# Chunked attention with a leaky-ReLU layer pair: two small VectorE operations in another form, value loads of two batches in pieces, and a new written order

## The chip, the cores and the metric

The kernel runs on one core of a Trainium2 chip. The time is that of the device for one launch, in microseconds, and the time of a kernel is the median of its runs. A profile is a separate, traced execution. The engines have these short names: PE is TensorE (PEld its weight loads), DVE is VectorE, ACT is ScalarE, POOL is GpSimd, SP is SyncE. In this kernel PE multiplies, DVE and ACT do the elementwise work, POOL does a part of it and issues the loads, and SP issues the stores and the DMA transposes.

## The reference

Eight batches of eight heads, 576 tokens and head dimension 64. Attention is local: each chunk of 64 tokens attends only to itself. The result, 4608 tokens by 512, goes through two matrix products with a leaky ReLU between them.

```
q_c, k_c, v_c = (t.reshape(B, H, 9, 64, 64) for t in (q, k, v))
scores = scale * np.matmul(q_c, k_c.transpose(0, 1, 2, 4, 3))
scores = scores - np.max(scores, axis=-1, keepdims=True)
attn = np.exp(scores)
attn = attn / (np.sum(attn, axis=-1, keepdims=True) + 1e-09)
out = np.matmul(attn, v_c)
x = out.transpose(0, 2, 1, 3).reshape(4608, 512)
h = x @ w_in          # 512 x 2048
g = np.maximum(0.01 * h, h)
return g @ w_out      # 2048 x 512
```

All numbers come in and go out as float32; the kernel computes in float16 with float32 sums.

## The kernel before

**Units and blocks.** Attention runs in 36 units of 128 tokens (two chunks, eight heads each); a unit is called u. The two products run in 19 blocks of tokens, called j: two of 128 tokens, then 17 of 256. The units feed a ring of transposed attention results, xT, and a block starts when its tokens are there. The second product of a block of 256 (and from block 14 on the first one too) is made by a scheme with seven products of half size instead of eight: that needs sums of inputs (SG, line 230, of the hidden values; TW, line 206, and WS, line 401, of the weights; xs, line 425, of the tokens) and sums of results (line 318).

**Stages of a unit.** Each unit passes through a chain. Its q and k come in (line 100), and are transposed: by PE for the first units, by DVE from unit 14 on, and by a DMA transpose that SP issues from unit 27 on (KT in line 843, QT in line 849; a DVE copy in line 856, stage cq, then spreads QT into the zero-padded tile QZ). Stage s (line 866) multiplies q and k into the scores Sp. Stage m (line 875) takes the maximum. Then there are two ways. Stages b and x subtract the maximum on DVE (line 880) and take one exponential on ACT (line 912). Stages nb and f scale the maximum by -1/8 on DVE (line 889) and take eight exponentials on ACT with that as their bias (line 897), which give the sums as well. UB lists the units from 14 on that go the first way. Stage z adds 1e-9 to the sums (line 924) and inverts them (line 926), stage n multiplies (line 932, on POOL from unit 10 on), stage d transposes the result by a DMA that SP issues (et, line 955), stage v multiplies by the values (line 966), and stage a (line 980, ACT) writes xT.

**Values.** The values of a batch lie in one of two tiles, VB0 and VB1, in every other block of a zero-padded square. The last unit that reads a batch issues the load of the batch after the next (lines 973 and 974), as two DMAs on POOL's queue.

**What sets the order.** Every engine executes its instructions in the order in which the program issues them; there is no scheduler behind it. For the first six units that order is written out in the string FRONT. It names stages and, as A and B, pieces of the first two blocks' products; as H their activation; as i matmuls on a tile of ones that fill waiting time; as y and w the zeroing of tiles. A third number after q, or a second one after k and c, says which of DVE and ACT makes the copy. Behind the front, the products are a list of pieces (chunks), issued one after the other; every other stage is an event with a due step, counted in pieces, which comes from base offsets (T and SPACE for the scores, VO for stage v, O_A and O_B for loads and DMA transposes) plus a shift from the table MOVED. Events that are due are issued ahead of the next piece. SG_POOL, XS_POOL and LEAK_DVE say which single sums and activations go to another engine than the usual one. Buffers come from rings: QT and q_in share a ring of five.

## Time and profile before

| what | value |
|---|---|
| median of 3 runs | 280.67 us (279.67 to 282.15) |
| the profiled execution's own time | 282.5 us |
| its span, first to last instruction | 280.7 us |
| PE busy | 270.9 us |
| DVE, ACT, POOL busy | 227.1, 190.3, 149.2 us |
| granted TensorE clock | 1.0 in all slices |

Times within the profile are counted from the start of the span. In a row of the order of time the first number is the start, the second the time taken, both in us, and a bracket at the end tells how long the engine stood idle ahead of the instruction and what ended that. Ends of matmuls are modelled, and a group of eight matmuls of 256 columns, listed with 1.04 us, is followed by the next group 0.87 us after its own start; the time that PE loses is therefore read from start to start. Rows of the table of stretches give busy time of PE, PEld, DVE, ACT and POOL, with the number of instructions, then the granted clock, the DMA share and GB/s.

### The profile page before, as it was taken

Reading aid. Unit: us, or ns where it says so; the run is one execution under the profiler, and the core shown is the slowest. Engines: PE = TensorE matmul, PEld = TensorE weight load, DVE = VectorE, ACT = ScalarE, POOL = GpSimd, SP = SyncE. Lnnn points to the kernel's source line nnn. Section 1 sums busy time; section 2 is a strip of 40 time slices with the busy share of each in tenths; the row PEclk is TensorE's granted clock in tenths of the full one; section 3 lists DMA queues with packets and bytes.
Section 4 is the critical chain, followed back from the end, with each engine's and each line's share of the span. In section 5 each row is a group of like instructions: output and inputs, shape, how many; then the busy total and the mean of one; then the engine's idle time right before and its main releaser. Section 6 shows DMA issues by size and latency. Waiting matters only on the chain.

```text
span 280.7 us, 8516 instructions
## 1 busy us (share of the span) xinstructions
PE 270.9 (96%) x3464; PEld 242.6 (86%) x3464; DVE 227.1 (81%) x453; ACT 190.3 (68%) x485; POOL 149.2 (53%) x176
## 2 busy tenths in 40 slices
PE   8889999999999999999999999999898999999995
PEld 4569958999999998999989999999788989999994
DVE  5876599899787988899968686779789989675684
ACT  6766734766657768657897646567566978976751
POOL 8838646879376696968232734268065472530000
PEclk9999999999999999999999999999999999999999
DMA  9999999999999999997919999999999423120213
GB/s 147 148 189 178 207 176 156 154 125 114 83 108 155 74 105 130 136 163 59 175 24 133 114 172 265 196 103 185 128 170 143 114 41 96 21 77 0 77 40 112
DMA packets 173958, 35.02 MB, mean 125 GB/s; under 512 B 164960, under 2 KB 169440, under 8 KB 173920
## 3 DMA queue, kind: packets, MB, share of 16 engines
q0 software_dynamic: 140256, 18.23, 113.2%
q1 hardware_dynamic: 32624, 16.00, 27.0%
q8 instruction: 27, 0.44, 0.6%
q10 hardware_dynamic: 1040, 0.26, 0.4%
q14 instruction: 11, 0.09, 0.1%
HBM read 36.96 MB, written 9.44 MB: 165 GB/s over the span
## 4 chain that ended last, share of the span: by engine, by line
PE 82%; DMA 8%; issue 4%; DVE 3%; POOL 2%; SPq 0%; POOLq 0%; DVEq 0%
PE hT L356 30%; PE prX L254 19%; PE prZ L254 6%; PE pr L254 6%; PE xbank L457 6%; PE xpr L457 4%; DMA VB<-in_v_dram 3%; PE prW L254 3%; PE Sp L866 3%; PE xp L966 3%; PE oP L503 2%; DMA k_in<-in_k_dram 2%; DMA et<-en 1%; DMA QT<-q_in 1%; DVE QZ L856 1%
## 5 line engine op out<-in xcount | busy, mean ns | idle before, releaser
L356 PE MATMUL hT<-xT,w_inT 128*128 128x256 f16 (+1 forms) x1088 | 103.1, 247 | 0.6 <-DMA w_inT<-in_moe_w_in_dram 0.6
L356 PEld LDWEIGHTS <-w_inT 128*128 128x128 f16 x1088 | 84.2, 98 | 7.2 <-issue 0.8
L370 ACT ACTIVATE gT<-hT 128x512 f16<-128x512 f32 x104 | 61.5, 605 | 26.2 <-PE hT L356 26.1
L932 POOL TENSOR_TENSOR en<-ex,zi 128x512 f16<-128x512 f16 x26 | 28.0, 1079 | 69.1 <-ACT gT L370 14.6
L254 PEld LDWEIGHTS <-SG 128*128 128x128 f16 x544 | 51.4, 98 | 5.4
L254 PEld LDWEIGHTS <-gT 128*128 128x128 f16 x400 | 37.7, 98 | 4.1
L254 PE MATMUL prX<-TW,SG 128*128 128x256 f16 x272 | 35.2, 273 | 0.0
L875 DVE TENSOR_REDUCE mx<-Sp 128x8 f32<-128x512 f32 x36 | 24.7, 685 | 12.2 <-PE Sp L866 12.0
L297 ACT ACTIVATE keep<-prX 128x256 f32<-128x256 f32 x51 | 19.9, 391 | 19.2 <-PE prX L254 18.9
L494 DVE TENSOR_TENSOR xkeep<-xpr,xkeep 128x512 f32<-128x512 f32 x30 | 19.9, 683 | 10.2 <-PE xpr L457 6.3
L100 POOL DMA_DIRECT2D q_in<-in_q_dram x25 | 21.1, 849 | 12.9 <-DMA QT<-q_in 6.4
L897 ACT ACTIVATE ex<-Sp,nb 128x64 f16<-128x64 f32 x80 | 24.0, 329 | 5.4 <-DVE nb L889 5.3
L980 ACT ACTIVATE xT<-xp 128x512 f16<-128x512 f32 x36 | 21.7, 602 | 5.5 <-PE xp L966 5.5
L100 POOL DMA_DIRECT2D k_in<-in_k_dram x25 | 20.6, 827 | 7.9 <-DMA VB<-in_v_dram 3.4
L230 DVE TENSOR_TENSOR SG<-gT 128x1024 f16<-128x1024 f16 x33 | 22.8, 692 | 1.0 <-ACT gT L370 0.8
L115 POOL DMA_DIRECT2D q_d<-in_q_dram x24 | 19.9, 830 | 2.2 <-DVE QZ L824 1.6
L486 ACT ACTIVATE xkeep<-xbank 128x512 f32<-128x512 f32 x30 | 16.8, 596 | 5.4 <-PE xbank L457 5.3
L115 POOL DMA_DIRECT2D k_d<-in_k_dram x24 | 19.5, 813 | 1.5 <-DMA k_d<-in_k_dram 1.1
L922 DVE TENSOR_REDUCE z<-ex 128x8 f32<-128x512 f16 x26 | 17.6, 677 | 2.9 <-ACT ex L912 2.6
L457 PEld LDWEIGHTS <-WS 128*128 128x128 f16 x320 | 19.3, 98 | 0.4
L122 POOL DMA_DIRECT2D VB<-in_v_dram x16 | 18.7, 1178 | 1.1 <-PE xp L966 1.1
L824 DVE STREAM_TRANSPOSE QZ<-q_d 64x512 f16<-64x512 f16 (+1 forms) x28 | 18.2, 655 | 0.3
(99 smaller groups left out, 486.9 us busy)
## 6 DMA issues: line engine op xcount, KB each, us to landing
out_dram<-osb SPq DMA_DIRECT2D x35, 256.0 KB, 3.5
VB<-in_v_dram POOLq DMA_DIRECT2D x16, 288.0 KB, 7.4
q_in<-in_q_dram POOLq DMA_DIRECT2D x19, 128.0 KB, 6.8
k_in<-in_k_dram POOLq DMA_DIRECT2D x19, 128.0 KB, 6.8
w_inT<-in_moe_w_in_dram POOLq DMA_DIRECT2D x8, 256.0 KB, 7.6
w_outT<-in_moe_w_out_dram POOLq DMA_DIRECT2D x4, 512.0 KB, 11.1
q_d<-in_q_dram POOLq DMA_DIRECT2D x24, 72.0 KB, 4.9
k_d<-in_k_dram POOLq DMA_DIRECT2D x24, 72.0 KB, 5.0
```

The source lines that it names most:

```text
L100: nc.gpsimd.dma_start(out=to, in_=rows)
L115: nc.gpsimd.dma_start(out=t[p0:p0 + 32, m, :, :, :].rearrange("p h b d -> p (h b) d"), in_=src[b, h0:h0 + 2, :, dh * 32:dh * 32 + 32].rear ...
L230: (nc.gpsimd if (j, n) in SG_POOL else nc.vector).tensor_tensor(out=SG[j, n], in0=x, in1=y, op=op)
L254: nc.tensor.matmul(out=to[:, i, :], lhsT=left[:, f, i * 128:(i + 1) * 128], rhs=right[:, f, :], start=(j, where) not in opened, stop=(f == ...
L297: nc.scalar.activation(out=half(kept[j, n]), in_=half(bank[j, "X"]), func=AFT.Copy, bias=0.0, scale=1.0)
L356: nc.tensor.matmul(out=hT[:, i, :], lhsT=w_inT[:, t, fc * 128:(fc + 1) * 128], rhs=xT[:, t, r0:r0 + tb], start=(t == 0), stop=(t == NT - 1),)
L370: nc.scalar.activation(out=gT[j][:, nf * a:nf * a + nf, c0:c0 + tb], in_=HT.pop((j, a, p)), func=AFT.Prelu, bias=0.0, scale=1.0, alpha=0.01,)
L457: nc.tensor.matmul(out=to[:, i, :], lhsT=left[:, t, i * 128:(i + 1) * 128], rhs=right[:, t], start=(n in (1, 2, 5) and t == 0 and i == 0), ...
L875: nc.vector.tensor_reduce(out=MX[u], in_=SP[u], axis=AXL.X, op=ALU.max)
L897: nc.scalar.activation(out=E[u][:, i, :], in_=SP[u][:, i, :], func=AFT.Exp, bias=NB[u][:, i:i + 1], scale=SCL, accum_out=Z[u][:, i:i + 1],)
L932: (nc.gpsimd if u >= UP else nc.vector).tensor_tensor(out=E[u], in0=ex, in1=ZI.pop(u).unsqueeze(2).to_broadcast((128, 8, CH)), op=ALU.mult)
L980: nc.scalar.activation(out=xT[:, :, at:at + G], in_=xp, func=AFT.Copy, bias=0.0, scale=1.0)
```

## The change

There are five parts.

1. Stage nb multiplies the maximum by a tile of 128x8 that holds -1/8 (minus), and stage z adds a tile that holds 1e-9 (tiny). Both were operations of a tensor and a number, and both are now operations of two tensors. Two small memsets at the start fill the tiles.
2. Unit 16 goes the first way (b, x) instead of the second (nb, f).
3. The values of batches 2 and 7 are loaded by four DMAs of half the size, as events of their own with the name vl, 2.5 steps apart and shifted by MOVED; the others are loaded as before.
4. The string FRONT is another one, and in the list of first loads unit 1 comes ahead of unit 2, and the fourth quarter of w_out ahead of the second.
5. The tables and offsets that set the due steps have other numbers. Two more sums SG go to POOL, the four xs of block 17 go from POOL to DVE, and two more activations go to DVE.

The added `need` and `made` lines are checks while the program is built; they issue nothing.

```diff
-    UB = (15, 17, 18, 19, 24, 25, 26, 27, 28, 30, 32, 34)
+    VL = (2, 7)
+    VS = 2.5
+    UB = (15, 16, 17, 18, 19, 24, 25, 26, 27, 28, 30, 32, 34)
...
+    def load_v_heads(b, m, h0, h1):
+        nc.gpsimd.dma_start(
+            out=VB[b % NVB][m * CH:(m + 1) * CH, h0:h1, :, m * CH:(m + 1) * CH].rearrange("p h c d -> p (h c) d"),
+            in_=v[b, m * H // 2 + h0:m * H // 2 + h1].rearrange("h (c j) d -> j (h c) d", j=CH),
+        )
...
+    tiny = sbp.tile([128, 8], FP32, name="tiny")
+    nc.vector.memset(tiny, 1e-9)
+    minus = sbp.tile([128, 8], FP32, name="minus")
+    nc.vector.memset(minus, -SCL)
...
-        "g2 g1 g3 v0 Q0 Q1 g4 Q2 Q3 g5 P0 P1 P3 P2 g6 v1 g7 g8 "
+        "g1 g2 g3 v0 Q0 Q1 g4 Q2 Q3 g5 P0 P3 P1 P2 g6 v1 g7 g8 "
...
-    MOVED = {..., 'WS 3': 3.25, 'd 30': 0.5, 'tdq 32': -0.5, 'tdq 33': 0.75, 'tdk 29': 0.25, 'tdk 33': 1.0, ...}
+    MOVED = {..., 'WS 3': 9.25, 'd 30': 6.25, 'tdq 32': 2.5, 'tdq 33': 5.25, 'tdk 29': 3.25, 'tdk 33': -1.5, ..., 'tdq 30': -3.0, 'vl 7 3': -2.0, 'vl 2 0': -1.0, ...}
-    SG_POOL = ((14, 1), (14, 4))
+    SG_POOL = ((14, 1), (14, 4), (16, 4), (17, 1))
...
-        nc.vector.tensor_scalar_mul(out=NB[u], in0=MX.pop(u), scalar1=-SCL)
+        nc.vector.tensor_tensor(out=NB[u], in0=MX.pop(u), in1=minus, op=ALU.mult)
...
-        nc.vector.tensor_scalar_add(out=ze, in0=z, scalar1=1e-9)
+        nc.vector.tensor_tensor(out=ze, in0=z, in1=tiny, op=ALU.add)
...
             if c == NCH - 1 and b + NVB < B:
-                load_v(b + NVB)
+                if b + NVB in VL:
+                    for i in range(4):
+                        later(i * VS, "vl", b + NVB, i)
+                else:
+                    load_v(b + NVB)
...
+    def load_v_piece(b, i):
+        made.add(("vl", b, i))
+        load_v_heads(b, i % 2, i // 2 * H // 4, i // 2 * H // 4 + H // 4)
...
 (FRONT, the pieces behind the first of block 0)
-  A0.0 H0.0 A1.0 e2 H1.0 A1.1 c2 v2 tq4 tk4 q4.0 H1.1 A0.1 a2 k4 H0.1 A2.0
+  A0.0 k3.1 z2 n2 A1.0 s3 H0.0 e2 c2 H1.0 A1.1 v2 A0.1 tq4 m3 tk4 H1.1 a2 A2.0
...
-    O_A = 12.0
-    O_B = 15.0
+    O_A = 10.0
+    O_B = 16.0
```

Three places of the order are shown, from the stretch between units 28 and 31. First POOL's, before the change: there en is a unit's attention (stage n), q_in and k_in are the loads of units 32 and 33, and VB1 is the load of batch 7.

```order
L100 DMA q_in_3756<-in_q_dram 128x8x64
L100 DMA k_in_3758<-in_k_dram 128x8x64
L932 TENSOR_TENSOR en_3787<-ex_3733,zi_3785 128x512
L122 DMA VB1_64<-in_v_dram 64x36x64 x2
L932 TENSOR_TENSOR en_3897<-ex_3831,zi_3883 128x512
L100 DMA q_in_3899<-in_q_dram 128x8x64
L100 DMA k_in_3901<-in_k_dram 128x8x64
L932 TENSOR_TENSOR en_4047<-ex_4015,zi_4032 128x512
```

With the change the same place on POOL reads so:

```order
L948 TENSOR_TENSOR en_3785<-ex_3733,zi_3783 128x512
L102 DMA q_in_3787<-in_q_dram 128x8x64
L102 DMA k_in_3789<-in_k_dram 128x8x64
L123 DMA VB1_64<-in_v_dram 64x18x64 x2
L948 TENSOR_TENSOR en_3887<-ex_3832,zi_3873 128x512
L123 DMA VB1_64<-in_v_dram 64x18x64
L102 DMA q_in_3912<-in_q_dram 128x8x64
L102 DMA k_in_3914<-in_k_dram 128x8x64
L123 DMA VB1_64<-in_v_dram 64x18x64
L948 TENSOR_TENSOR en_4049<-ex_4015,zi_4033 128x512
```

The load of unit 32 has moved behind the attention of unit 28, and the values stand in four rows of half the size, the third ahead of and the fourth behind the load of unit 33.

Second SP's queue, before the change, up to the transpose of k of unit 33; et is a unit's transposed attention (stage d: units 28, 29 and 30 here), osb2 a store of results, and the first KT and QT are those of unit 31.

```order
L330 DMA out_0_dram<-osb2_3714 128x512
L330 DMA out_0_dram<-osb2_3689 128x512
L955 DMA_TRANSPOSE et_3811<-en_3787 128x4x128
L843 DMA_TRANSPOSE KT_3813<-k_in_3614 128x4x128
L849 DMA_TRANSPOSE QT_3837<-q_in_3611 128x4x128
L955 DMA_TRANSPOSE et_3903<-en_3897 128x4x128
L843 DMA_TRANSPOSE KT_3979<-k_in_3758 128x4x128
L849 DMA_TRANSPOSE QT_3994<-q_in_3756 128x4x128
L330 DMA out_0_dram<-osb2_3992 128x512
L955 DMA_TRANSPOSE et_4091<-en_4047 128x4x128
L330 DMA out_0_dram<-osb2_3895 128x512
L843 DMA_TRANSPOSE KT_4141<-k_in_3901 128x4x128
```

With the change:

```order
L344 DMA out_0_dram<-osb2_3718 128x512
L860 DMA_TRANSPOSE KT_3777<-k_in_3629 128x4x128
L344 DMA out_0_dram<-osb2_3691 128x512
L971 DMA_TRANSPOSE et_3811<-en_3785 128x4x128
L866 DMA_TRANSPOSE QT_3813<-q_in_3626 128x4x128
L971 DMA_TRANSPOSE et_3899<-en_3887 128x4x128
L860 DMA_TRANSPOSE KT_3993<-k_in_3789 128x4x128
L866 DMA_TRANSPOSE QT_4035<-q_in_3787 128x4x128
L344 DMA out_0_dram<-osb2_3988 128x512
L860 DMA_TRANSPOSE KT_4064<-k_in_3914 128x4x128
L344 DMA out_0_dram<-osb2_3885 128x512
L971 DMA_TRANSPOSE et_4180<-en_4049 128x4x128
```

The transpose of k of unit 31 has moved ahead of a store and of unit 28's attention, and that of k of unit 33 and a store now stand ahead of unit 30's attention. Further ahead, the two transposes of unit 30 have moved before unit 27's attention.

Third DVE, before the change, up to the copies of QT of unit 31 (COPY QZ1); mx and Sp are those of unit 30.

```order
L401 TENSOR_TENSOR WS3_3937<-w_inT_68 128x2x512 x2
L425 TENSOR_TENSOR xs_3951<-xT_70 128x256
L875 TENSOR_REDUCE mx_3962<-Sp_3953 128x8
L401 TENSOR_TENSOR WS4_3964<-w_inT_68,WS2_3843 128x2x512 x2
L425 TENSOR_TENSOR xs_3951<-xs_3951,xT_70 128x256
L880 TENSOR_TENSOR Sp_3953<-Sp_3953,mx_3962 128x512
L318 TENSOR_TENSOR osb2_3992<-prZ_3920,keep_3990 128x256
L425 TENSOR_TENSOR xs_3951<-xT_70 128x256
L856 COPY QZ1_66<-QT_3837 64x8x64 x2
```

With the change:

```order
L416 TENSOR_TENSOR WS3_3951<-w_inT_68 128x2x512 x2
L416 TENSOR_TENSOR WS4_3954<-w_inT_68,WS2_3842 128x2x512 x2
L891 TENSOR_REDUCE mx_3966<-Sp_3957 128x8
L332 TENSOR_TENSOR osb2_3988<-prZ_3922,keep_3986 128x256
L896 TENSOR_TENSOR Sp_3957<-Sp_3957,mx_3966 128x512
L440 TENSOR_TENSOR xs_3991<-xT_70 128x256
L873 COPY QZ1_66<-QT_3813 64x8x64 x2
L440 TENSOR_TENSOR xs_3991<-xs_3991,xT_70 128x256
```

Both sums of weights now stand ahead of the maximum of unit 30, and one sum xs stands ahead of the copies instead of three. On PE the scores of unit 31 have moved one piece ahead and stage v of unit 29 one piece back; stages v of units 6, 8, 9, 13, 19, 23 and 25 stand one to three pieces earlier, and those of units 20, 27 and 28 one piece later.

More of the change, by code (lines that the diff above doesn't have):

```diff
@@ L216, in token_sums @@
             return
+        if j in EARLY:
+            for a, p in {
+                1: [(a, 1) for a in range(4)], 2: [(0, 2), (1, 2)], 3: [(0, 1), (1, 1), (0, 2), (1, 2)], 4: [(2, 2), (3, 2)],
+            }[n]:
+                need("act", j, a, p)
         if n in (2, 4):
@@ L794, in stage_q @@
             of = of.rearrange("p i e (r j) -> p (i e) r j", r=2)
+        need("zero", u % NQZ)
+        made.add(("dq", u, s))
         if act:
@@ L960, in stage_v @@
     def stage_v(u):
+        for i in range(2):
+            need("zero", NQZ + 2 * ((2 * u + 1) // NCH % NVB) + i)
         et = ET.pop(u)
@@ L972, in stage_v @@
                 )
+            if b in VL:
+                for i in range(4):
+                    need("vl", b, i)
             if c == NCH - 1 and b + NVB < B:
-                load_v(b + NVB)
+                if b + NVB in VL:
+                    for i in range(4):
+                        later(i * VS, "vl", b + NVB, i)
+                else:
+                    load_v(b + NVB)
         XP[u] = xp
+    def load_v_piece(b, i):
+        made.add(("vl", b, i))
+        load_v_heads(b, i % 2, i // 2 * H // 4, i // 2 * H // 4 + H // 4)
     def stage_a(u):
@@ L1007, in second_layer @@
     def second_layer(j, p):
+        need("act", j, p, 0)
         chunks.remove(("mm2", j, 0, p))
```

32 lines of the change are left out of this document (16 added, 16 removed), and 14 rows, old and new, of the table FRONT.

## The prediction

> **What bounds the kernel now.** I read the busy times first, then stretches of the span, then the order of time on PE, and from each wait there back to DVE, SP and POOL.
>
> ```profile
> PE 270.9 (96%) x3464; PEld 242.6 (86%) x3464; DVE 227.1 (81%) x453; ACT 190.3 (68%) x485; POOL 149.2 (53%) x176
> ```
>
> ```profile
> 100.00:120.00 20.00, 20.00 (x221) 18.07 (x220) 17.86 (x34) 13.64 (x39) 17.15 (x21) 1.00 2.43 138
> 200.00:220.00 20.00, 17.50 (x247) 15.93 (x245) 16.25 (x36) 14.67 (x42) 9.75 (x12) 1.00 1.31 141
> 240.00:260.00 20.00, 20.00 (x276) 18.74 (x274) 12.91 (x25) 15.44 (x32) 6.19 (x9) 1.00 0.11 35
> 270.00:281.00 11.00, 7.50 (x81) 6.65 (x78) 6.40 (x13) 2.58 (x6) 0.00 (x0) 1.00 0.28 97
> ```
>
> PE works 96% of the span at the full granted clock, and in the stretches 100 to 120 and 240 to 260 it never stops. So the kernel is PE's list of pieces plus the places where PE stands still: the front, the stretch 200 to 220, and the last three microseconds, when the products are done and only additions and stores are left. The change leaves PE's products as they are (one filler matmul more), so it can gain only at places where PE stands still, and it loses wherever it makes a new one. In the stretch 200 to 220 PE's order of time shows three stops.
>
> ```profile
> 201.18 1.04 PE L356 MATMUL hT<-xT,w_inT 128*128 128x256 f16 x8
> 203.37 0.41 PE L866 MATMUL Sp<-KT,QZ 128*128 128x64 f16 x8 [1.16 <-DVE QZ L856]
> 204.32 0.41 PE L966 MATMUL xp<-et,VB 128*128 128x64 f16 x8 [0.54 <-DMA et<-en]
> ...
> 211.63 1.04 PE L254 MATMUL prZ<-TW,SG 128*128 128x256 f16 x8
> 213.47 0.41 PE L866 MATMUL Sp<-KT,QZ 128*128 128x64 f16 x8 [0.80 <-DVE QZ L856]
> ```
>
> Eight matmuls of 256 columns hold PE for 0.87 us and eight of 64 columns for 0.24. From start to start the scores of unit 31 therefore lose 203.37 - 201.18 - 0.87 = 1.32, stage v of unit 29 loses 204.32 - 203.37 - 0.24 = 0.71, and the scores of unit 32 lose 213.47 - 211.63 - 0.87 = 0.97: 3.0 us together. The first and the third wait for the copies of QT (line 856), the second for the transposed attention et. Next, what DVE waited for there, and SP's queue.
>
> ```profile
> 200.58 0.29 DVE L425 TENSOR_TENSOR xs<-xT 128x256 f16<-128x256 f16 x1
> 202.73 0.59 DVE L856 COPY QZ<-QT 64x512 f16<-64x512 f16 x2 [1.86 <-DMA QT<-q_in]
> ...
> 211.60 1.81 DVE L856 COPY QZ<-QT 64x512 f16<-64x512 f16 x2
> ```
>
> ```profile
> 190.33 1.22 SPq L955 DMA_TRANSPOSE et<-en  x1
> 191.72 1.25 SPq L843 DMA_TRANSPOSE KT<-k_in  x1
> 193.14 1.27 SPq L849 DMA_TRANSPOSE QT<-q_in  x1
> 194.88 1.62 SPq L955 DMA_TRANSPOSE et<-en  x1
> ...
> 205.75 1.20 SPq L955 DMA_TRANSPOSE et<-en  x1
> 207.04 0.53 SPq L330 DMA_DIRECT2D out_dram<-osb  x1
> 207.67 1.81 SPq L843 DMA_TRANSPOSE KT<-k_in  x1
> ```
>
> ```profile
> 186.61 0.95 POOL L100 DMA_DIRECT2D q_in<-in_q_dram  x1 [1.52 <-DMA QT<-q_in]
> ...
> 190.26 2.37 POOL L122 DMA_DIRECT2D VB<-in_v_dram  x2
> ```
>
> ```profile
> QT<-q_in SPq DMA_TRANSPOSE x9, 4.6
> ```
>
> The transpose QT of unit 31 was issued at 193.14 and DVE got it at 202.73, 9.6 us later, against a median of 4.6 for its kind. The et of unit 29 went out at 194.88 and released PE at 204.32, 9.4 us later. Both follow the value load of batch 7, issued at 190.26. So the hole is a load of values that stands in the way of transposes which PE needs soon.
>
> **The change part by part.** All times are in the clock of the profiled execution: its span of 280.7, and 1.8 around it to its own 282.5. That is 1.8 above the median of 280.67, so I take the sum as a difference and subtract it from the median.
>
> *The front.* Its rows on PE:
>
> ```profile
> 20.00 0.39 PE L940 MATMUL tpe<-ident,en 128*128 128x128 f16 x4
> 20.77 1.05 PE L356 MATMUL hT<-xT,w_inT 128*128 128x128 f16 x16 [0.38 <-DMA w_inT<-in_moe_w_in_dram]
> 21.66 0.40 PE L966 MATMUL xp<-et,VB 128*128 128x64 f16 x8
> 21.89 0.39 PE L771 MATMUL qp<-ident,q_in 128*128 128x128 f16 x4
> 22.57 0.38 PE L771 MATMUL kp<-ident,k_in 128*128 128x128 f16 x4 [0.29 <-DMA k_in<-in_k_dram]
> ```
>
> The start of the hidden products is set by loads (w_in at 20.77, k of unit 4 at 22.57), and those loads keep their places in the queue; the swaps are of equal sizes. So whatever is reordered before 20.77 costs and brings nothing as long as it is done by then: the scores of unit 3 now stand in the wait ahead of 20.77. The transposes of q and k of unit 4 now stand behind the piece A0.1, so the stop 22.57 - 21.89 - 0.23 = 0.45 has work in it. Bounds: -0.45, and 0 if the attention of unit 2, which now has one copy of k more ahead of it on DVE, comes late instead. I take -0.35. From there to 200, PE stops nowhere, so this gain is carried.
>
> *The hole.* The transposes of unit 31 are due about one and a half steps earlier. KT now stands ahead of unit 28's attention, so that QT follows the latter's issue (190.33 + 1.22) at about 191.6 in place of 193.14, and behind it only half of the values have been put in the queue. If QT takes as long as before, 9.6, it lands at 201.2; with the median of 4.6 it lands at 196.2. DVE had reached this point at 200.58 + 0.29 = 200.87 and loses two of the three small sums ahead of it, so the copies can run from 200.3 and end at 200.9. The scores now stand one piece ahead, at 201.18 of the old clock less the front's 0.35, that is 200.8. Their loss is then 0.1 to 1.2; I take 0.2, near the median's end, because the copies need QT only at 200.3, 8.7 us after its issue: 1.1 less than before.
>
> Stage v of unit 29 goes behind two pieces: 200.8 + 0.2 + 0.24 + 2 x 0.87 = 203.0. Its et goes out as before at 194.88 less 0.35, because its attention on POOL does; with 9.4 it comes at 203.9 and costs 0.9, with less it costs nothing. I take 0.3 in place of 0.71.
>
> The scores of unit 32 come 7.1 after the next pieces' start on PE's list, in both kernels. The copies ahead of them took 1.81 for what takes 0.59 above. Their chain begins with the scores of unit 31 and runs over nb, so all of it moves up by the same 2.4 or so; without the 1.2 of slowness they don't hold PE, with it they hold it as before. I take 0.25 in place of 0.97, as the copies now come before POOL's sums of the tokens of block 15, which wait for the attention of unit 29.
>
> New costs: the et of unit 28 has a transpose more ahead of it in SP's queue, but it is used one piece later; and the et of unit 30 stands behind the load of k of unit 33. I put 0.2 for both, from 0 to what the slow rival below gives.
>
> *The two-tensor forms.* These rows bound them:
>
> ```profile
> 220.40 1.29 DVE L889 TENSOR_SCALAR nb<-mx 128x8 f32<-128x8 f32 x1
> ...
> 249.56 1.12 DVE L230 TENSOR_TENSOR SG<-SG,gT 128x1024 f16<-128x1024 f16 x1
> ```
>
> ```profile
> L230 DVE TENSOR_TENSOR SG<-gT 128x1024 f16<-128x1024 f16 x33 | 22.8, 692 | 1.0 <-ACT gT L370 0.8
> ```
>
> ```profile
> 219.54 2.12 POOL L230 TENSOR_TENSOR SG<-gT 128x1024 f16<-128x1024 f16 x1
> ...
> 249.47 0.66 POOL L425 TENSOR_TENSOR xs<-xT,xs 128x256 f16<-128x256 f16 x1
> ```
>
> The nb at 220.40 took 1.29 and ended when POOL's sum ended (221.66). If the new form never waits, this saves at most about 1.1 at that place. But the sum at 249.56, already an operation of two tensors in SBUF, ran 1.12 beside a POOL operation as well, 0.4 more than the mean of 0.69 of the sums like it. So I take 0 for the edit on PE's path. The Trainium skill, page "SBUF — State Buffer", section "Who interferes with whom", says of this that a VectorE instruction with two SBUF inputs contends with a GpSimd instruction that reads SBUF, though not with one that only writes it; by that rule the new form escapes descriptor writing alone, the sum stays as it is, and the trace agrees (1.12 at 249.56).
>
> *The rest.* Unit 16 on the other way gives DVE two more operations over a unit's scores and takes seven operations from ACT; it lies near 105, where DVE has 20 - 17.86 = 2.1 us to spare, room for two of up to 1 us each, and PE never stops: 0. The value load of batch 2 in pieces is read 30 us later: 0. The moves in blocks 16 and 17 lie where DVE is busy 12.91 of 20: 0. If that cover fails, the new sum on POOL (2.12 by the row above, against 0.69) holds up block 18's sums by up to 1.4; I leave it in the range.
>
> Sum: -0.35 (front) - 1.1 - 0.4 - 0.7 (hole) + 0.2 = -2.35. From its own time 282.5 that is 280.15, from the median 280.67 it is 278.3.
>
> **The rivals.** *All stops close.* With the median latency the hole's 3.0 and the front's 0.45 go whole and nothing new comes: 280.67 - 3.45 = 277.2, and somewhat less if later small stops go too. For it: 4.6 is the usual. Against it: loads of unit 32 now fall into the same stretch.
>
> *The crowd stays.* The load of unit 32 was issued at 186.61 and now follows the attention of unit 28, at 190.3, into the crowd, which is what half the values have left. QT then lands as before, at 202.73 - 0.35, its copies end at 203.0, and the scores, now one piece ahead, stop PE for 2.2 in place of 1.32; stage v loses nothing (-0.71), unit 32 loses as before: -0.35 + 0.9 - 0.7 = -0.15, so 280.5.
>
> *Slower: SP stands still for k of unit 33.* Its transpose (207.67 before, behind the et of unit 30 at 205.75) now stands ahead of that et, and its load stands behind three of the four value pieces. Stage v of unit 30 reads that et here:
>
> ```profile
> 216.37 0.40 PE L966 MATMUL xp<-et,VB 128*128 128x64 f16 x8
> ```
>
> In the new clock that is 216.37 - 2.5 = 213.9. Issued behind the transpose (1.81) and a store (0.53), and with QT's 4.6 to land, the et is late once the transpose goes out after 207.0; the gain is eaten once it goes out after 209.3. If the load comes 3 us later than 207.67, PE stops there for 3.7, and the sum is +1.35: 282.0. Against it: at 207.67 at the latest that load had landed, with all four pieces ahead.
>
> *The front or a moved stage v slips.* Seven stages v stand 0.87 to 2.6 earlier, and the front's DVE chain is fuller. One stop of 1.2 gives 279.5.
>
> **How the numbers follow.** Chances: the forecast 0.50 (own range 277.2 to 279.4), all stops close 0.17, the crowd stays 0.15, SP stands still 0.10, a stage slips 0.08. The likeliest gives 278.3. The range from 276.6 to 281.0 takes in all but the slow rival and the ends of the others. One per cent, about what a measurement can tell here (the three runs spread over 0.9%), is 2.8 us: faster than 277.86 are two fifths of the forecast's cases and the first rival, 0.36; slower than 283.5 are half of the slow rival's cases and a few of the last, 0.07; the rest, 0.57, is within.
>
> **What would show it.** The hole's step is right if the scores of unit 31 and 32 and stage v of unit 29 show waits under 0.3 each, and QT of unit 31 is there when DVE comes. It is wrong if DVE again waits over 1 us for QT. The front is right if no transposition of k waits near 22. The slow rival shows as a wait of stage v for et near 214 behind a late KT in SP's queue. The two-tensor step is wrong if nb never takes over 0.3 beside POOL's sums. The whole is wrong if PE loses more than 0.5 at any place between 25 and 195.

## The result, and the profile after

The changed kernel takes 279.13 us, the median of 20 runs (278.31 to 280.82); the kernel before, run beside it on the same chip, 281.72 (20 runs, 279.67 to 285.39). The ratio is 0.9915, with a 95% interval of 0.9892 to 0.9937: 1.8 to 3.0 us less. That is within one per cent, the most likely of the three outcomes in the prediction. The profiled execution of the changed kernel has a time of 279.04 and a span of 277.3; 280.7 was the span before. So the two profiles lie 3.4 apart and the medians 2.6; where the 0.8 comes from is seen below.

The busy times, and the four stretches that the prediction reads (length, busy time of PE, PEld, DVE, ACT and POOL, granted clock, DMA share, GB/s):

```profile
PE 269.9 (97%) x3465; PEld 242.7 (88%) x3465; DVE 227.9 (82%) x460; ACT 186.9 (67%) x468; POOL 153.6 (55%) x178
```

```profile
100.00:120.00 20.00, 20.00 (x215) 18.04 (x214) 17.93 (x35) 11.91 (x23) 15.79 (x19) 1.00 2.36 136
200.00:220.00 20.00, 19.90 (x289) 18.38 (x288) 17.88 (x40) 18.05 (x57) 11.38 (x12) 1.00 1.16 151
240.00:260.00 20.00, 19.94 (x276) 18.68 (x274) 15.73 (x28) 13.57 (x28) 7.23 (x6) 1.00 0.23 58
270.00:277.30 7.30, 4.04 (x45) 3.55 (x43) 3.24 (x9) 0.77 (x2) 0.00 (x0) 1.00 0.30 108
```

From 200 to 220 PE now works 19.90 of 20 where it worked 17.50. At 100 and at 240 it does not stop, as before, and the end (products done, stores left) is as long as it was. The hole on PE's order of time in the changed kernel, with the rows that answer to those of the prediction:

```profile
199.39 1.04 PE L268 MATMUL prX<-TW,gT 128*128 128x256 f16 x8
200.41 0.41 PE L882 MATMUL Sp<-KT,QZ 128*128 128x64 f16 x8
...
202.40 0.40 PE L984 MATMUL xp<-et,VB 128*128 128x64 f16 x8
...
208.82 1.04 PE L268 MATMUL prZ<-TW,SG 128*128 128x256 f16 x8
209.96 0.41 PE L882 MATMUL Sp<-KT,QZ 128*128 128x64 f16 x8
```

No row names a releaser any more. From start to start the scores of unit 31 lose 200.41 - 199.39 - 0.87 = 0.15 (1.32 before), stage v of unit 29 at 202.40 nothing (0.71), the scores of unit 32 209.96 - 208.82 - 0.87 = 0.27 (0.97). The transposes behind this, in the list of DMA issues with the median time to landing in us, each taken in a window that holds only itself: of the kernel before the et of unit 28 (issued at 190.33), QT of unit 31 (193.14) and the et of unit 29 (194.88):

```profile
et<-en SPq DMA_TRANSPOSE x1, 5.9
QT<-q_in SPq DMA_TRANSPOSE x1, 9.6
et<-en SPq DMA_TRANSPOSE x1, 9.4
```

The same three in the changed kernel, issued at 189.08, 190.47 and 194.27:

```profile
et<-en SPq DMA_TRANSPOSE x1, 5.4
QT<-q_in SPq DMA_TRANSPOSE x1, 5.9
et<-en SPq DMA_TRANSPOSE x1, 5.8
```

QT of unit 31 is there at 196.3 and DVE comes for it at 199.77; the et of unit 29 is there at 200.1, 2.3 us ahead of its use. On DVE in the changed kernel, the copies of QT of units 31 and 32, and nb of unit 33:

```profile
199.77 0.58 DVE L873 COPY QZ<-QT 64x512 f16<-64x512 f16 x2
...
208.86 1.04 DVE L873 COPY QZ<-QT 64x512 f16<-64x512 f16 x2
...
216.89 1.27 DVE L905 TENSOR_TENSOR nb<-mx,minus 128x8 f32<-128x8 f32 x1
```

And POOL, the first two rows beside the copies of unit 32, the third beside nb:

```profile
208.12 0.88 POOL L102 DMA_DIRECT2D k_in<-in_k_dram  x1
209.08 0.67 POOL L440 TENSOR_TENSOR xs<-xT 128x256 f16<-128x256 f16 x1
...
216.02 2.12 POOL L244 TENSOR_TENSOR SG<-gT 128x1024 f16<-128x1024 f16 x1
```

The first of the two copies of unit 32 took 0.27, from 208.86, and slipped in as POOL's load ended (209.00) and before its sum began (209.08); the second took 0.75, as long as the sum. Before, the first had met the sum as well (1.07 and 0.72).

**A measure without the front's spread.** All profiles in this text start their products at other times, so here are differences of start times on PE within each: the first hidden product; from it to the first piece of block 2, the third block that starts (A2.0 in FRONT, called the third group here); from the scores of unit 30 to those of unit 33, which hold the hole, and from there to the scores of unit 34; from there to the last product. The runs below are in it.

| kernel | first product at | to third group | scores 30 to 33 | 33 to 34 | 34 to the last |
|---|---|---|---|---|---|
| before | 18.22 | 5.46 | 22.90 | 7.98 | 49.22 |
| changed | 17.85 | 5.03 | 20.30 | 7.97 | 49.29 |
| pieces alone | 20.09 | 4.79 | 20.95 | 7.98 | 49.08 |
| KT 31 early alone | 18.19 | 5.21 | 22.56 | 7.98 | 49.24 |
| pieces, KT 31 early | 17.42 | 5.00 | 24.36 | 7.99 | 49.19 |
| no load of batch 7 | 17.63 | 5.08 | 21.69 | 7.99 | 49.24 |
| pieces, new SP and POOL rows | 19.01 | 5.14 | 20.94 | 7.97 | 49.19 |
| new SP and POOL rows, whole load | 17.78 | 5.41 | 21.09 | 7.97 | 49.23 |
| changed, whole load | 18.03 | 4.95 | 20.31 | 7.98 | 49.05 |
| changed, number forms | 18.31 | 5.01 | 20.30 | 7.98 | 49.09 |
| front alone | 18.74 | 4.86 | 22.13 | 7.98 | 49.28 |
| changed, copies early | 18.21 | 5.00 | 20.02 | 7.53 | 49.21 |
| before, pieces and copies | 18.47 | 5.33 | 19.91 | 7.53 | 49.25 |
| changed, et 28 late | 19.23 | 4.71 | 25.13 | 7.97 | 49.07 |

Between before and changed the column of the hole falls by 2.60. The columns behind it hardly move, and the stretch between the third group and the scores of unit 30, which has no column, takes 196.34 - 18.22 - 5.46 = 172.66 before and 195.43 - 17.85 - 5.03 = 172.55 with the change. So the unit on the other way, the values of batch 2, the moved stages v and the moves in blocks 16 and 17 together cost nothing and bring 0.1 at most; no run takes them one by one.

### The profile page after: what moved, and what is told of

Read it like the earlier page. It is cut to its first block, busy times and chain, and to the rows that moved or that the text cites. A ratio compares the mean times of both kernels' runs of the same rounds, so it can differ in the third digit from the quotient of the medians.

```text
span 277.3 us, 8516 instructions
## 1 busy us (share of the span) xinstructions
PE 269.9 (97%) x3465; PEld 242.7 (88%) x3465; DVE 227.9 (82%) x460; ACT 186.9 (67%) x468; POOL 153.6 (55%) x178
## 4 chain that ended last, share of the span: by engine, by line
PE 79%; DVE 7%; DMA 6%; POOL 3%; ACT 2%; issue 1%; DVEq 0%; ACTq 0%; POOLq 0%
PE hT L370 30%; PE prX L268 18%; PE pr L268 6%; PE prZ L268 5%; PE xbank L472 5%; DMA w_inT<-in_moe_w_in_dram 4%; PE xpr L472 3%; PE Sp L882 3%; PE prW L268 3%; PE xp L984 3%; PE oP L518 2%; ACT ex L913 2%; DVE SG L244 2%; DMA et<-en 2%; DVE QZ L873 1%
## 5 line engine op out<-in xcount | busy, mean ns | idle before, releaser
L244 DVE TENSOR_TENSOR SG<-gT 128x1024 f16<-128x1024 f16 x32 | 23.4, 730 | 1.1 <-ACT gT L384 1.0
L913 ACT ACTIVATE ex<-Sp,nb 128x64 f16<-128x64 f32 x72 | 21.5, 332 | 1.9 <-DVE nb L905 1.8
L123 POOL DMA_DIRECT2D VB<-in_v_dram x20 | 21.0, 1062 | 1.0 <-PE xp L984 0.9
L938 DVE TENSOR_REDUCE z<-ex 128x8 f32<-128x512 f16 x27 | 18.3, 677 | 2.2 <-ACT ex L928 1.9
```

The source lines that it names most:

```text
L123: nc.gpsimd.dma_start(out=VB[b % NVB][m * CH:(m + 1) * CH, h0:h1, :, m * CH:(m + 1) * CH].rearrange("p h c d -> p (h c) d"), in_=v[b, m * ...
L244: (nc.gpsimd if (j, n) in SG_POOL else nc.vector).tensor_tensor(out=SG[j, n], in0=x, in1=y, op=op)
L913: nc.scalar.activation(out=E[u][:, i, :], in_=SP[u][:, i, :], func=AFT.Exp, bias=NB[u][:, i:i + 1], scale=SCL, accum_out=Z[u][:, i:i + 1],)
```

## The experiments

Times are medians; "ratio" is against the kernel before on the same chip, with its 95% interval. A stop that a row shows is given as its bracket has it, some 0.17 less than from start to start. In the first four the question is what closes the hole: the pieces, an earlier QT, or both.

**Pieces alone.** Base: the kernel before.

```
+    VL = (7,)
+    VS = 2.5
...
-                load_v(b + NVB)
+                if b + NVB in VL:
+                    for i in range(4):
+                        later(i * VS, "vl", b + NVB, i)
+                else:
+                    load_v(b + NVB)
```

> The kernel before, with one thing taken from the change: the value load of batch 7 goes out in four pieces, two at once and two after the attention of unit 29. The order of SP's transposes and of PE stays as before. Theory A (the hole is made by what stands in the DMA queues ahead of QT of unit 31 and et of unit 29; pieces and an earlier QT each take a part): QT is issued at about 193.1 as before, with half of the bytes ahead of it, and lands between 199 and 200.5 in place of 202.7; DVE comes at 200.9, so the stop before the scores of unit 31 falls from 1.32 to under 0.4, et of unit 29 lands near 202 to 203 and costs under 0.4; 1.0 to 2.0 us less than the kernel before. Theory B (the order of SP's queue is what counts, pieces of the same bytes change nothing): QT lands after 202 again, the stops stay at 3.0 us together and the time within 0.4 us of the kernel before.

Measured: 281.02 us (279.34 to 281.93), ratio 0.9933 (0.9898 to 0.9968). QT of unit 31 and the et of unit 29, in the list of issues:

```profile
QT<-q_in SPq DMA_TRANSPOSE x1, 6.4
et<-en SPq DMA_TRANSPOSE x1, 6.9
```

On PE the scores of units 31 and 32:

```profile
203.51 0.40 PE L871 MATMUL Sp<-KT,QZ 128*128 128x64 f16 x8
...
212.97 0.41 PE L871 MATMUL Sp<-KT,QZ 128*128 128x64 f16 x8 [0.84 <-DVE QZ L861]
```

Theory A. Though issued in the old order, both transposes come in 6 to 7 us in place of 9.5, and the two stops that they made (1.32 and 0.71) are gone: 20.95 in place of 22.90 in the table. The third, DVE's copies beside POOL, stays at 0.84 (0.80 before).

**An earlier KT of unit 31 alone.** Base: the kernel before.

```
-'tdk 31': 0.25
+'tdk 31': -1.75, 'tdq 31': -0.5
```

> The kernel before, with one thing taken from the change: the transpose KT of unit 31 stands ahead of the et of unit 28 in SP's queue, so that QT of unit 31 goes out about 1.4 us earlier, at 191.7. The value load of batch 7 goes out whole as before. Theory A: most of the value load is still ahead of QT; it lands between 199.5 and 201.5, the stop before the scores of unit 31 falls from 1.32 to 0 to 0.7, but et of unit 29 still lands near 204 and now holds PE there for what the scores gave back; 0 to 0.5 us less than the kernel before. Theory B (the order of SP's queue counts): QT lands by 197, the stop goes whole, and with it 1.0 to 2.0 us of the time.

Measured: 282.15 us (280.41 to 286.61), ratio 0.9991 (0.9955 to 1.0028). No gain, as theory A has it, but by a way that neither names. The et of unit 28 and QT of unit 31 in the list of issues:

```profile
et<-en SPq DMA_TRANSPOSE x1, 8.2
QT<-q_in SPq DMA_TRANSPOSE x1, 9.8
```

PE stopped for the first of them, before stage v of unit 28:

```profile
199.40 0.39 PE L966 MATMUL xp<-et,VB 128*128 128x64 f16 x8 [0.93 <-DMA et<-en]
```

With KT ahead of it the et of unit 28 went out at 191.14, 1.6 us behind the first issue of the value load (189.58), and took 8.2. Before it went out 0.07 behind that issue and took 5.9. In this trace the hole had only found another victim.

**Both of these.** Base: the kernel before; the two diffs above together.

> The kernel before with both things taken from the change and nothing else of it: the value load of batch 7 in four pieces, and KT of unit 31 ahead of the et of unit 28 in SP's queue. Theory A: as in the changed kernel QT of unit 31 lands before 198, the stop before its scores falls under 0.2, et of unit 29 lands near 201 to 203, stage v of unit 29 waits under 0.3, and the copies of unit 32 no longer take 1.8; 1.8 to 2.5 us less than the kernel before, which is all of the hole's gain. Theory C (the gain needs the moved stages too: stage v of unit 29 behind two pieces and the copies of unit 32 ahead of POOL's sums): the stops at unit 31 and unit 29 go, but that at unit 32 (0.97) stays, and the time falls by 0.8 to 1.5 us.

Measured: 281.32 us (280.10 to 284.30), ratio 0.9966 (0.9933 to 0.9999). The gain is 0.3 us smaller by the medians than that of the pieces alone, but the intervals overlap. In the trace neither theory holds. The same et again, and its stop; then the stretches of PE around it:

```profile
199.24 0.55 PE L971 MATMUL xp<-et,VB 128*128 128x64 f16 x8 [2.02 <-DMA et<-en]
```

```profile
198.00:200.00 2.00, 0.77 (x10) 0.64 (x10) 1.99 (x7) 0.78 (x2) 0.00 (x0) 0.83 2.60 118
200.00:202.00 2.00, 2.00 (x11) 1.40 (x10) 1.16 (x4) 0.89 (x2) 0.54 (x1) 0.50 1.95 159
202.00:204.00 2.00, 2.00 (x17) 1.63 (x16) 0.00 (x0) 0.73 (x3) 2.00 (x3) 0.82 2.13 179
```

The et of unit 28 went out at 190.38, 1.7 us behind the first piece (188.70), and took 8.8. QT of unit 31 was there at 199.4, well ahead of its copies. After the stop of 2.02 the granted clock fell to 0.50. But this trace is not the usual execution: it took 282.67, and ten of the twelve runs show a mean granted clock of 0.998 or more, which leaves no room for such a drop (it makes 0.994). So the 24.36 in the table is a bad case. An earlier QT that delays the transpose which has to go out ahead of the load shows no gain in the runs, and harm in these two traces.

**Without the load.** Base: the kernel before; the values of batch 7 aren't loaded.

```
-            if c == NCH - 1 and b + NVB < B:
+            if c == NCH - 1 and b + NVB < B - 1:
```

> The kernel before without the value load of batch 7 (left out of the computation: the values of batch 7; its units are computed with values of an earlier batch that lie in the same buffer). It measures what the load costs in the hole. Theory A: with nothing of it in the queues QT of unit 31 lands within 4 to 6 us of its issue (by 198.5), et of unit 29 by 200.5, the stops before the scores of unit 31 and stage v of unit 29 go (1.32 and 0.71), and that of unit 32 falls as well or stays at most at 0.97; 2.0 to 3.0 us less than the kernel before. Rival D (the transposes are slow by themselves there, since three of them and the loads of units 32 and 33 stand in the queue): QT still takes over 8 us, and the time falls by under 0.5 us.

Measured: 280.61 us (279.08 to 281.97), ratio 0.9940 (0.9914 to 0.9967). QT of unit 31 comes in 3.8 us, the et of unit 29 in 5.8, and the two stops go:

```profile
QT<-q_in SPq DMA_TRANSPOSE x1, 3.8
et<-en SPq DMA_TRANSPOSE x1, 5.8
```

Rival D falls: it is the load that makes these transposes slow. By the ratios, what the load costs in the kernel before is what the pieces get back, 1.7 us here (1.9 there). It is a little less than expected, since the stop at unit 32 (0.83) stays and a new one of 0.45 comes at 207.09, for ACT.

**Pieces, with the change's rows of SP and POOL.** Base: pieces alone. The order on PE and DVE stays old; SP and POOL read between 175 and 215 as in the changed kernel.

```
-O_A = 12.0, O_B = 15.0; 'tdk 29': 0.25, 'tdq 29': 1.25, 'tdk 33': 1.0, 'tdq 33': 0.75, 'tdq 32': -0.5, 'd 30': 0.5, 'd 31': 4.0
+O_A = 10.0, O_B = 16.0; 'tdk 29': 3.25, 'tdq 29': 1.0, 'tdk 33': -1.5, 'tdq 33': 5.25, 'tdq 32': 2.5, 'd 30': 6.25, 'd 31': 3.75, 'tdq 30': -3.0, 'tdk 32': 1.5, 'vl 7 3': -2.0
```

> The kernel before with the value load of batch 7 in four pieces and with all of the change's moves in SP's and POOL's rows between 175 and 215 (the transposes of units 29 to 33, the attention of unit 28 on POOL ahead of the load of unit 32); the order on PE, DVE and ACT stays as before. In the run with the pieces and KT of unit 31 alone in its new place, et of unit 28 fell 1.7 us behind the first piece, took 8.8 us to land in place of 5.4 to 6, and PE stopped 2.02 us for it. Theory A (a transpose that goes out ahead of a load's first piece is quick, one that goes out over a microsecond behind it is slow): here, with SP's row ahead of time, et of unit 28 goes out ahead of the pieces and lands within 6 us, QT of unit 31 lands by 198, the stops before the scores of unit 31 and before stages v of units 28 and 29 are each under 0.2, and only the stop at unit 32 (0.8, DVE's copies beside POOL) stays: 1.5 to 2.3 us less than the kernel before. Theory C (the gain needs the new order on PE and DVE too): a stop of over 0.7 shows at one of these three places and the time is less than 1.0 us below the kernel before.

Measured: 280.62 us (279.26 to 282.00), ratio 0.9941 (0.9907 to 0.9975). Here the et of unit 28 goes out at 190.64, ahead of the first piece (191.71), and DVE's copies of unit 32 are as slow as ever:

```profile
et<-en SPq DMA_TRANSPOSE x1, 5.6
```

```profile
210.17 1.79 DVE L861 COPY QZ<-QT 64x512 f16<-64x512 f16 x2
```

Theory A: 20.94, the same as with the pieces alone, and only the stop at unit 32 (0.84) is left. One expectation failed: QT of unit 31, issued 0.3 us behind the first piece, took 7.7 us and was there at 199.74, not by 198; DVE came for it later still. With KT of unit 31 early the et of unit 28 must still go out ahead of the load, which is what the change's rows bring about.

**The change's rows with the whole load.** Base: the run before; `VL = ()`.

> The kernel before with the change's rows of SP and POOL between 175 and 215 as in the run before, but with the value load of batch 7 whole; PE, DVE and ACT keep their old order. Counted from the scores of unit 30 to those of unit 33 on PE, which leaves out the spread of the front, the kernel before took 22.90 (22.1 to 22.9 in three profiles with its stretch), the pieces alone 20.95, the pieces with the new rows 20.94, the changed kernel 20.30. Theory A (two remedies for one illness: the pieces, or transposes that go out ahead of the load; either is enough): 20.9 to 21.5, QT of unit 31 lands by 200.5, no stop over 0.5 but that at unit 32; 1.2 to 2.2 us of time below the kernel before. Theory B (in the old order of PE the whole load still stands in the way): 22.0 or more, with a stop for QT of unit 31 or et of unit 29.

Measured: 280.27 us (280.03 to 281.16), ratio 0.9946 (0.9920 to 0.9972). QT of unit 31, issued 0.2 us behind the load's first issue, and the et of unit 29:

```profile
QT<-q_in SPq DMA_TRANSPOSE x1, 6.6
et<-en SPq DMA_TRANSPOSE x1, 7.7
```

Theory A: 21.09 without any piece, with 0.30 left at stage v of unit 29. The pieces and the order on SP and POOL are two remedies, and either is enough. What SP's part and POOL's part do singly was not run.

**The changed kernel with the whole load.** Base: the changed kernel; `VL = (2,)`, so that only the load of batch 2 is in pieces.

> The changed kernel with one part undone: the value load of batch 7 goes out whole again, in two DMAs of 1.2 us issue time each, where the first piece stood. Theory A (what counts is the bytes ahead of a transpose in the DMA queues): QT of unit 31, issued at 190.5 between the two, lands at 197 to 200, just in time for DVE at 199.8; et of unit 29, issued at 194.3 behind all of it, lands at 203 to 204.5 in place of 200.1, against stage v at 202.4: a stop of 0.6 to 2.0 us, and the time 0.6 to 2.0 above the changed kernel, so 0.4 to 1.8 below the kernel before. Theory B (the new order on SP closes the hole by itself): no new stop, within 0.3 us of the changed kernel.

Measured: 279.95 us (279.01 to 280.46), ratio 0.9921 (0.9886 to 0.9957); the changed kernel 0.9915. The scores of unit 31 and stage v of unit 29, and QT of unit 31 and the et of unit 29:

```profile
200.57 0.41 PE L882 MATMUL Sp<-KT,QZ 128*128 128x64 f16 x8
...
202.56 0.40 PE L984 MATMUL xp<-et,VB 128*128 128x64 f16 x8
```

```profile
QT<-q_in SPq DMA_TRANSPOSE x1, 6.5
et<-en SPq DMA_TRANSPOSE x1, 7.2
```

Theory B for this kernel: 20.31 against 20.30. The load whole makes the et of unit 29 1.4 us slower, but it lands at 201.7 and its stage v stands at 202.56. I had expected it after 203.

**The number forms again.** Base: the changed kernel.

```
-        nc.vector.tensor_tensor(out=NB[u], in0=MX.pop(u), in1=minus, op=ALU.mult)
+        nc.vector.tensor_scalar_mul(out=NB[u], in0=MX.pop(u), scalar1=-SCL)
...
-        nc.vector.tensor_tensor(out=ze, in0=z, in1=tiny, op=ALU.add)
+        nc.vector.tensor_scalar_add(out=ze, in0=z, scalar1=1e-9)
```

> The changed kernel with one part undone: nb and ze are operations of a tensor and a number again. Theory A (the waits that the new form removes lie beside descriptor writing on POOL, at places where DVE does not hold PE): the longest ze goes back from 0.17 to over 0.5 us, nb still takes up to 1.3 us beside POOL's sum in both forms, and the time stays within 0.4 us of the changed kernel, 2.0 to 2.8 below the kernel before. Rival (the small operations stand on the chain from scores to scores and each of their waits is paid): 0.6 us or more above the changed kernel, with new stops of PE before scores or stage v.

Measured: 279.63 us (279.15 to 280.78), ratio 0.9912 (0.9878 to 0.9945), 20.30 in the table: 0, theory A. Shortest, median and longest of nb and ze in ns, here:

```profile
L905 DVE TENSOR_SCALAR nb<-mx x9: 165/290/1292, 93.1 to 233.4; 128x8 f32<-128x8 f32 x9
L940 DVE TENSOR_SCALAR ze<-z x36: 151/172/221, 11.3 to 237.4; 128x8 f32<-128x8 f32 x36
```

and in the changed kernel:

```profile
L905 DVE TENSOR_TENSOR nb<-mx,minus x9: 161/166/1275, 92.6 to 232.9; 128x8 f32<-128x8 f32 x9
L940 DVE TENSOR_TENSOR ze<-z,tiny x36: 156/167/169, 10.7 to 236.9; 128x8 f32<-128x8 f32 x36
```

Both forms take 1.3 us beside POOL's sum. The new form takes nb's median from 290 to 166; ACT waits a little less for it (1.8 us in three places, 2.2 in five with the number form), and PE gains nothing by it. One expectation failed: ze went back only to 0.22, not to the 0.55 of the kernel before, as in the new order it hardly meets POOL's descriptor writing any more.

**The front alone.** Base: the kernel before, with `FRONT` and the two swaps in `LOADS`.

> The kernel before with one part of the change alone: the new order of the front and of the two swapped pairs of loads. The first hidden product began at 18.2, 18.2, 17.4 and 17.6 us in four profiles of the old front, and at 17.9 in the changed kernel, so that much of the 0.8 us that the two profiles differ by at 45 us may be the loads' own spread. Theory A (the front's gain is the stop for k of unit 4, 0.45 at most): counted from the first hidden product, the third group of them (A2.0, 5.0 to 5.5 behind it with the old front) comes 5.0 behind, no stop of 0.2 or more between; the time is 0 to 0.5 us below the kernel before, which lies within what the runs can tell. Rival (the new front brings the whole 0.8): 0.8 us or more below, with the first hidden product itself earlier than in all of the old profiles.

Measured: 282.14 us (280.41 to 284.48), ratio 1.0001 (0.9964 to 1.0038). The third group comes 4.86 behind the first product, as theory A has it, and the rival falls. The hole in this run, where nothing of its code had changed:

```profile
202.45 0.41 PE L866 MATMUL Sp<-KT,QZ 128*128 128x64 f16 x8 [0.40 <-DVE QZ L856]
203.80 0.41 PE L966 MATMUL xp<-et,VB 128*128 128x64 f16 x8 [0.95 <-DMA et<-en]
```

Stops of other sizes than in the profile of before, and 22.13 in place of 22.90: the hole differs by 0.8 between these two traces of the same code, which is as much as the two profiles lie farther apart than the medians.

**The copies out of POOL's way.** Base: the changed kernel.

```
-'cq 32 0': 1.5, 'cq 32 1': 3.0, 'cq 34 0': 1.5, 'cq 34 1': 0.75, 'z 31': -0.75
+'cq 32 0': -2.75, 'cq 32 1': -2.75, 'cq 34 0': -1.5, 'cq 34 1': -1.5, 'z 31': -0.5
```

> The changed kernel with the copies of QT of units 32 and 34 on DVE taken out of the places where POOL works beside them: those of unit 32 stand behind the sums of block 13, in 0.95 us that DVE waits there, those of unit 34 three operations earlier. Theory A (such a copy takes as long as POOL's instruction beside it, 0.75 and 1.03 in place of 0.29, and PE stops 0.10 and 0.27 for it): all four copies take under 0.35, the stops before the scores of units 32 and 34 go, 20.05 to 20.2 us from the scores of unit 30 to those of unit 33 and 7.7 to those of unit 34 (20.30 and 7.97 before), 0.3 to 0.6 less in all. Rival (QT of unit 32 comes too late for the new place, or something else stops PE there): the same sums, or more.

Measured: 279.19 us (277.73 to 280.54), ratio 0.9902 (0.9872 to 0.9932). The copies of units 32 and 34:

```profile
204.90 0.60 DVE L873 COPY QZ<-QT 64x512 f16<-64x512 f16 x2
...
220.43 0.58 DVE L873 COPY QZ<-QT 64x512 f16<-64x512 f16 x2
```

Theory A: 0.58 to 0.60 a pair, where those of unit 32 took 1.04 and those of unit 34 1.34, and the table falls by 0.28 and 0.44. The gain of 0.7 shows in the trace; the runs cannot tell it from none.

**The two small edits.** Base: pieces alone, with the same moves of the copies ('z 31' at -1.0).

> The kernel before with two small edits only: the value load of batch 7 in four pieces, and the copies of QT of units 32 and 34 earlier on DVE; front, SP's row, PE's order and the other moves as before. Theory A (all that the change brings in its stretch is had from these two): 20.0 to 20.3 us from the scores of unit 30 to those of unit 33 (22.90 in the kernel before, 20.95 with the pieces alone, 20.30 in the changed kernel), 2.2 to 3.2 us of time below the kernel before, no slower than the changed kernel by more than the front's 0.2 to 0.5. Rival (the other moves are needed for unit 32): 20.6 or more and under 2.0 us.

Measured: 279.26 us (278.55 to 279.69), ratio 0.9901 (0.9879 to 0.9924). Scores of unit 32, without a stop:

```profile
211.04 0.40 PE L871 MATMUL Sp<-KT,QZ 128*128 128x64 f16 x8
```

Theory A: 19.91 and 7.53, a little under the changed kernel with the copies moved (20.02 and 7.53). With the old front, the old order on SP and POOL and the old forms, two edits of the kernel before give all that the change gives, and the intervals of the three overlap. No version measured here is shown to beat the changed kernel.

**A long stop.** Base: the changed kernel.

```
-'d 28': 0.25
+'d 28': 9.0
```

> The changed kernel with the transpose et of unit 28 behind that of unit 29 in SP's queue, so that it goes out at about 195.5 in place of 189.1 and PE stops for it before stage v of unit 28 (198.3). It prices a stop of over two microseconds. In the run with pieces and KT of unit 31 alone a stop of 2.02 was followed by a granted clock of 0.50 for some 4 us; after stops of 0.9 to 1.4 it stayed at 1.00. Theory A (a stop of 2 us or more costs about as much again in clock): et lands at 200 to 202, PE stops for 2 to 4 us, the granted clock falls to 0.5 behind it for 3 to 5 us, and the time is 3.5 to 6 us above the changed kernel. Rival (the low clock there was chance): the clock stays at 1.00 and the time is above the changed kernel by the stop alone, 1.5 to 3.5.

Measured: 284.51 us (281.02 to 285.07), ratio 1.0077 (1.0045 to 1.0109), 5.3 above the two runs just told. The stop, and the stretches behind it:

```profile
203.04 0.39 PE L984 MATMUL xp<-et,VB 128*128 128x64 f16 x8 [3.43 <-DMA et<-en]
```

```profile
202.00:204.00 2.00, 0.96 (x13) 0.79 (x13) 0.94 (x4) 0.00 (x0) 0.94 (x1) 0.86 1.65 197
204.00:206.00 2.00, 2.00 (x11) 1.44 (x10) 0.00 (x0) 0.96 (x2) 1.88 (x3) 0.50 0.08 5
206.00:208.00 2.00, 2.00 (x23) 1.70 (x22) 0.86 (x2) 1.02 (x4) 0.00 (x0) 0.78 1.50 96
```

The clock does fall, so the rival is out, but theory A has its price too high. The hole's column rises by 4.83 (25.13 - 20.30), of which stage v of unit 28 accounts for 3.60 (6.45 behind the scores of unit 30 in place of 2.85). The other 1.2 is the clock's. Nine of the ten runs have a mean granted clock of 0.994 or less; the tenth, with 1.000, took 281.02.

## Why the prediction was right, and where not

**The sum.** It forecast -2.35; measured are -2.6 by the medians. The forecast of 278.3 was counted from the three runs known then (280.67), and more runs of the kernel before put it at 281.72, so 279.13 is higher than forecast while the gain is a little larger.

**What bounds the kernel** was right: the change gains where PE stood still, and 0.1 at most elsewhere. The end of the table's row, from the scores of unit 33 on, differs by 0.06.

**The front** (-0.35) was about right in size and can't be proved by time. The stop for k of unit 4 is gone in the changed kernel and in the front alone. With the old front the third group came 5.00 to 5.46 behind the first product, leaving out the run with a slow start, and with the new one 4.71 to 5.03, the 4.71 again in a run that started late; on the means about 0.3. The first product itself, which the profiles put at 0.37 earlier, is not the change's: with one and the same old front it came at 17.42 to 20.09.

**The hole** (-2.0 with the new costs of 0.2) lies between what the profiles show, -2.60 against the profile of before and -1.83 against the other with its stretch untouched (22.13); its cause was half named. Scores of unit 31: taken 0.2, measured 0.15. Stage v of unit 29: taken 0.3, measured 0. Scores of unit 32: taken 0.25, measured 0.27. The reason "a load of values that stands in the way of transposes" is shown by the run without the load. One reading in its working is off: from the issue of QT to DVE's coming there were 200.87 - 193.14 = 7.7 us before, so the 8.7 with the change is 1.0 more room, not "1.1 less"; the 0.2 holds all the same. The step that failed is the one that made both moves share the work ("behind it only half of the values have been put in the queue"). The pieces alone close the two stops, and the rows of SP and POOL alone nearly do (21.09 without any piece, 20.95 with the pieces alone); in the changed kernel the pieces are a reserve, 2.3 us of margin for the et of unit 29 in place of 0.9.

**"The et of unit 28 has a transpose more ahead of it"** was put, with another, at 0.2 and cost nothing, but the reason given was not what decides. It is used one piece later, which gives 0.9; behind the load it comes 2.8 to 3.4 later (8.2 and 8.8 us in place of 5.4). It was free because it goes out at 189.08, ahead of the load. A good part of that is POOL's doing: with the change the load of unit 32 stands between unit 28's attention and the values.

```profile
187.47 1.04 POOL L948 TENSOR_TENSOR en<-ex,zi 128x512 f16<-128x512 f16 x1 [4.26 <-ACT osb L330]
188.46 0.95 POOL L102 DMA_DIRECT2D q_in<-in_q_dram  x1
...
190.27 1.74 POOL L123 DMA_DIRECT2D VB<-in_v_dram  x2
```

The attention ends at 188.51 and the values follow 1.76 us later. With KT of unit 31 alone moved they followed at once (189.52 and 189.58), the et went out 1.6 behind the load, and in the traces this term was a stop of 0.93, and of 2.02 with the pieces. The prediction listed no such rival, and its rival "the crowd stays" counted this very move on POOL as harm.

**The copies of unit 32** came early enough by 0.1 us for one of the two. "Without the 1.2 of slowness they don't hold PE" was right, as the run with the copies moved shows.

**The two-tensor forms** (0 on PE's path) were right: undone, they change nothing. The Trainium skill, page "SBUF — State Buffer", section "Who interferes with whom", has the new form contend with a reading GpSimd instruction all the same; nb of unit 33 agrees, 1.27 beside POOL's sum. The same section says that a copy of VectorE in its fast two-port mode and a GpSimd instruction hold each other off whole. The copies of QT agree, if they are of that mode: 0.28 alone, 1.07 in the kernel before beside a load's descriptor writing and a sum.

**The rivals.** SP did not stand still: k of unit 33 was there at 201.9, its transpose went out at 202.56 and the et of unit 30 at 204.47, in time. The crowd did not stay, though the load of unit 32 moved into it. That all stops close is nearly what happened in the hole. The slow rival's price was too low: it put 3.7 us of standing still into the sum without a clock that falls behind it.

## What to carry to other kernels

If a wait for a DMA is long only sometimes, list for each transfer how far behind the first issue of the big load it went out: here the et of unit 28 took 4.7 to 6.0 us wherever it went out ahead of the load or within 0.1 us of its first issue, QT of unit 31 took 5.9 to 7.7 where it went out 0.2 to 0.6 behind, and transposes 1.5 to 6 us behind a whole load took 7.2 to 9.8. So the lag sorts them roughly, not exactly. Moving one transfer ahead moves another behind, so look who becomes the last. And try the parts of a change alone before keeping them all: two small edits gave the same time as the whole change.

## What the runs showed of the hardware

**A stop of PE of 2 us can cost more than itself.** After stops of 2.02 and 3.43 us the granted clock was 0.50 for about 3.4 us each: from the stretches above, (1.00 - 0.83 + 1.00 - 0.50 + 1.00 - 0.82) x 2 / 0.5 = 3.4, and likewise 3.4 for the second. In the second this cost 1.2 us of PE's time. After stops of 0.93, 1.16 and 1.41 (the last ahead of the first product in the run with pieces and the new rows of SP and POOL) it stayed at 1.00. The size of one stop is not the whole rule: in every trace here the stretches at one clock that lie within the span last 3.41 us or a whole multiple of it (in the second case from 203.45 to 206.86), so where a stop falls in that grid may count too, which was not tried. The Trainium skill, page "TensorE: Matmul & The Clock Gate", section "What's actually happening", says that the clock halves after an idle window of about 3.4 us and comes back after as long a busy one. The way back agrees with the trace (3.4); a stop of 2.02 that was enough does not, and the measurement decides.

**The front's clock can be low as well.** In the run with the pieces alone the granted clock was 0.60 from 10 to 15 us and 0.72 from 15 to 20, and the first product came at 20.09. The run with the front alone has a stretch at 0.50 from 13.77 us, that with the late et of unit 28 one from 15.72, and in none of the three had PE stopped for longer than 0.8 us at a time ahead of it. What sets it off there was not tried.

**A copy can take three times its length without a wait in its row.** A pair of copies of 0.58 took 1.79 where POOL wrote descriptors and then added, and the rows show no idle time for it: it is seen only against the same operation elsewhere.
